# The first pair's z in 32-row products, with the stack for the rest sent by DMA

## Chip, cores and metric

One core of one Trainium2 chip. The metric is the device time of one execution in microseconds (us). Names of engines: PE is TensorE's matmul stream and PEld its weight loads, DVE is VectorE, ACT is ScalarE, POOL is GpSimd, SP is SyncE, which here only issues DMAs.

## What is computed

Three layers in a row; only the third is touched by the change, and the second hands it its input.

```python
x = attention(q, k, v)                       # 2304 rows of 512
# second layer, "moe": 8 experts x 4 slots
logits = x @ phi                             # 2304 x 32
slot_input = softmax_over_rows(logits).T @ x # 32 x 512
slot_out[e] = relu(slot_input[e] @ w1[e]) @ w2[e]
x = softmax_over_slots(logits) @ slot_out    # = c @ slot_out
# third layer, "moe2": 8 experts, every row through every expert
P = exp(x @ w_gate - max); 8 rounds of row and column normalisation
for e in range(8):
    out += P[:, e:e+1] * (relu(x @ w1[e]) @ w2[e])
```

## The kernel before

The input of the third layer is never formed. Since x = c @ slot_out, the product x @ m1[e] is c @ (slot_out @ m1[e]): `prep_w1(e)` multiplies the transposed slot outputs `st` (32 columns) into m1[e], scales the 32 x 1024 result by a power of two and splits it into two f16 parts, `sh` (high) and `sl` (low). These lie as 128 x 256: four groups of 32 partitions (kk), each with 256 of the 1024 columns. `stk[e]`, the stack, is 128 x 1024 f16: rows sh, sh, sl, sl of 32 each, which is the operand that PE loads as weights. `ct` holds the split and transposed c in the matching row order (hi, lo, hi, lo), so that one 128-row product sums all four cross products. `emit_z(m, fh)` makes z for a pair m of row tiles (n and n + 9) and half fh of the 1024 columns: 4 matmuls of 256 columns into a PSUM tile of two banks.

For e of 1 and more the stack is filled by 16 small DMAs from SP (L765, 32 partitions x 512 B each). For e = 0 it is made on PE: 8 products with selection matrices `selh`, `sell` (L774), 3 idle products (L777), and four copies out of PSUM by ACT and DVE (L779).

After z, each pair has seven products (Strassen style): `hi_z`, `lo_z`, `relu_z`, `sum_z`, `hi_s` and `lo_s` read z (or sums of it) and write the f16 operands `ops`; `prod` is then 12 matmuls of 256 columns (L1149) over one operand. The order on PE is written out by hand: for pair 0 it is KA11 (high part), KA12 (high part), KA11 (low part), the matmuls of `first_w1` (m1[1], L721), KA12 (low part), KS2, z of pair 1 (first half), KS3, z of pair 1 (second half), KS1, KA22, then KA11 of pair 1, KS4 of pair 0, and so on. `left(m + 1, k_)` puts the work of ACT, DVE and POOL on the next pair behind step k_ of this one; `side` does the same for the preparation of the next expert: `magnitude(1)` with eight ACT passes over m2[1] (L605), `prep_w1(1)`, the gate and its normalisation. Every engine takes its instructions in this order. `add` on ACT copies x out of PSUM between two products that accumulate in the same x, so the later product waits for that copy.

Loads come by SP alone. `load_part` sends 2 MB of m1[1] and of m2[1] into `wraw` (L67) as the last two loads ahead of the main loop. The tile framework puts all semaphores, those of the DMAs' landings included.

The lines that the change touches: L491 to L501 (`constants`), L716 to L781 (`prep_w1`), L890 to L895 (`ct_turn`), L947 to L980 (end of the second layer and `prep_w1(0)`), L996 to L1000 (`gate`), L1255 to L1325 (start of the main loop).

Of the kernel before, what the change touches and what calls it, by code (L numbers as in the profile page):

```python
# [26 lines left out]
def tile_kernel(ctx: ExitStack, tc: tile.TileContext, q, k, v, phi, w1, w2, w_gate, m1, m2, rel, out):  # L27
    nc = tc.nc
# [71 lines left out]
    with tc.manual_schedule():  # L100
        with ExitStack() as ab:
# [8 lines left out]
            with ExitStack() as at:  # L110
# [380 lines left out]
                id16, selh, sell = [ring[:, 8, 256 + 64 * i:320 + 64 * i].bitcast(F16) for i in range(3)]  # L491

                def constants():
                    nc.gpsimd.tensor_copy(out=id16, in_=idn)
                    nc.gpsimd.memset(selh, 0.0)
                    nc.gpsimd.memset(sell, 0.0)
                    for i in range(4):
                        for cp in range(4):
                            dst = selh if cp < 2 else sell
                            nc.gpsimd.tensor_copy(out=dst[32 * i:32 * i + 32, 32 * cp:32 * cp + 32],  # L500
                                                  in_=idn[32 * i:32 * i + 32, 32 * i:32 * i + 32])  # L501
# [91 lines left out]
            bound = {}  # L593

# [121 lines left out]
            def prep_w1(e, ps=None, pool=None, beside=None, behind=None, last=None):  # L716
# [22 lines left out]
                ar = mp.tile([128, 1], F32, tag="ar1", name="ar1")  # L739
                nc.vector.tensor_reduce(out=ar, in_=ps[:, 256:384 if e else 385], axis=AX.X, op=ALU.max)  # L740
# [5 lines left out]
                if e == 0:  # L746
                    last(0)
                nc.vector.tensor_single_scalar(inv_s[:, e:e + 1].bitcast(I32), ar.bitcast(I32), 0x7F800000,
                                               op=ALU.bitwise_and)
# [5 lines left out]
                if e == 1:  # L755
                    yield
                nc.vector.scalar_tensor_tensor(out=sl, in0=ps[:, 0:256], scalar=iv, in1=sh,
                                               op0=ALU.mult, op1=ALU.subtract)
                yield
                yield  # L760
                stk[e] = (sp if e % 2 else mp).tile([128, F], F16, tag="stk", name="stk", bufs=1)
                if e:
                    for i, part in enumerate((sh, sh, sl, sl)):
                        for kk in range(4):
                            nc.sync.dma_start(out=stk[e][32 * i:32 * i + 32, 256 * kk:256 * kk + 256],  # L765
                                              in_=part[32 * kk:32 * kk + 32, :])
                    yield
                    return
                last(1)
                pss = [pool.tile([128, 512], F32, tag="b", name="m") for _ in range(4)]  # L770
                for lhs, rhs in ((selh, sh), (sell, sl)):
                    for kk in range(4):
                        rows = slice(32 * kk, 32 * kk + 32)
                        nc.tensor.matmul(pss[kk][:, 0:256], lhsT=lhs[rows], rhs=rhs[rows], start=lhs is selh,  # L774
                                         stop=lhs is sell, tile_position=(32 * kk, 0))
                for _ in range(3):
                    nc.tensor.matmul(pss[3][:, 256:512], lhsT=id16, rhs=ct.rearrange("p a b -> p (a b)")[:, 0:256], start=True, stop=True)  # L777
                for kk in range(4):
                    (nc.vector.tensor_copy if kk % 2 else nc.scalar.copy)(  # L779
                        out=stk[e][:, 256 * kk:256 * kk + 256], in_=pss[kk][:, 0:256])  # L780
                yield  # L781

            with ExitStack() as bs:
# [106 lines left out]
                def ct_turn(g, copy=nc.vector.tensor_copy):  # L890
                    n = min(4, NT - 4 * g)
                    ps = pb.tile([128, 4, 128], F16, tag="b", name="bc")
                    for i in range(n):
                        nc.tensor.transpose(ps[:, i, :], ct[:, 4 * g + i, :], id16)
                    return lambda: copy(out=ct[:, 4 * g:4 * g + n, :], in_=ps[:, 0:n, :])  # L895
# [9 lines left out]
                for e in range(E):  # L905
                    mm1(e)
                    for _ in range((2, 4, 2, 2, 0, 1, 0, 0)[e]):
                        next(p2)
                    if e == 0:
                        slots()  # L910
                    if e == EH - 1:
                        tr1_out(0)
                    if e == EH + 1:
                        for g in range(NG):
                            ct_split(g)
                    if e == EH + 2:
# [30 lines left out]
                for h in range(2):  # L947
                    for fc in range(FC):
                        mm2(E - 1, fc, h)
                    (nc.scalar.copy if h else nc.vector.tensor_copy)(  # L950
                        out=s2b[:, 256 * h:256 * h + 256], in_=s2[h][:, 0:256])
                pc = pm.tile([128, 512], F32, name="m")
                turned, later = [], []
                for h in range(2):
# [6 lines left out]
                    if h == 0:  # L961
                        turned.append(ct_turn(0))
                turned.pop()()

                def beside():
                    turned.append(ct_turn(2))
                    later.append(cn_turn(pc, 0, 2))

                def behind():
                    turned.pop()()  # L970
                    turned.extend((ct_turn(1, nc.scalar.copy), ct_turn(3), ct_turn(4)))
                    later.append(cn_turn(pc, 2, 4))
                    later.append(cn_turn(s2[0][:, 256:512], 4, 5))
# [5 lines left out]
                for _ in prep_w1(0, ph, pb, beside, behind, last):  # L979
                    pass  # L980
# [3 lines left out]
            with ExitStack() as ms:  # L984
# [9 lines left out]
                def gate():  # L994

                    st4 = sp.tile([128, DC, 4, NS], F32, name="st4")  # L996
# [3 lines left out]
                    nc.vector.tensor_copy(out=st4, in_=st.unsqueeze(2).to_broadcast([128, DC, 4, NS]))  # L1000
# [65 lines left out]

                def emit_z(m, fh):
                    e, n = divmod(m, NP)
                    if fh == 0:
                        pool = wcv if m % 2 == 0 else wone  # L1070
                        ops_[m] = pool.tile([128, 7, 2, 4, 128], F16, tag="w", name="ops")
# [183 lines left out]
                load_part("m1", 1, wraw, 0, 1)  # L1255
                load_part("m2", 1, wraw, 0, 1)
                emit_z(0, 0)
                emit_z(0, 1)
# [13 lines left out]
                lo_z(0, KA12, 1, 2)  # L1272
                xt[0] = px.tile([128, 256], F32, tag="x", name="x")
# [6 lines left out]
                hi_s(0, KS3, "s3")  # L1280
                lo_s(0, KS3, "s3")
                lo_s(0, KS2, "s2", nc.vector)
                sum_z(0, "s1", 2, 2, "r21", ALU.add)
                sum_z(0, "s4", 1, 2, "s2", ALU.subtract)
                prod(0, KA12, yt[0][:, 0], True, (1,))
                side = None
                for m in range(NM):
# [12 lines left out]
                    for k_ in range(7):  # L1300
# [18 lines left out]
                        if k_ == 0:  # L1319
                            if m:  # L1320
                                last(m - 1)
                            left(m, 7)
# [72 lines left out]
```

## Time and profile before

| | us |
|---|---|
| median of 3 runs | 909.25 (908.68 to 910.03) |
| the profiled execution | 909.3 |
| its span, first to last instruction | 907.5 |
| PE busy | 894.7 (99%) |
| DVE, ACT, POOL busy | 673.3, 583.1, 562.6 |

The stretch that the change touches lies between 151 us, where the second layer's last matmul ends, and 180 us. Times of rows are counted from the start of the span. From about 177 us on, PE runs without a gap to the end, so an amount by which that point moves is an amount by which the end moves.

### The profile page before, as it was taken

How to read it: one execution, taken by the hardware profiler on the slowest of the kernel's cores; microseconds unless marked ns; L12 is line 12 of the kernel's file. 1: busy time of each engine (PE TensorE's matmuls, PEld its weight loads, DVE VectorE, ACT ScalarE, POOL GpSimd, SP SyncE). 2: the span in 40 equal slices, each digit the busy share in tenths (PEclk: the TensorE clock that was granted, in tenths of full speed). 3: DMA queues.
4: the chain of work that ended last, by engine and by line, in shares of the span. 5: the costliest groups of instructions: out<-in, count | busy, mean ns of one | idle time of the engine just before them, and what ended most of it. 6: DMA issues, size and time to landing. Idle time of an engine off the chain costs nothing.

```text
span 907.5 us, 24182 instructions
## 1 busy us (share of the span) xinstructions
PE 894.7 (99%) x9604; PEld 772.2 (85%) x9604; DVE 673.3 (74%) x1627; ACT 583.1 (64%) x1322; POOL 562.6 (62%) x716
## 2 busy tenths in 40 slices
PE   8999999999999999999999999999999999999998
PEld 6777765888888888888888888888888888888887
DVE  6666668688867777777787778777777777777775
ACT  7777655767768785766476656665666666664442
POOL 2111233458865996598659874997489848894452
PEclk9999999999999999999999999999999999999999
DMA  9999999120022002300230023001300020002222
GB/s 299 357 333 325 323 410 423 65 99 1 2 98 101 1 1 97 104 1 2 94 105 2 2 93 106 1 1 58 142 1 2 17 90 2 2 1 48 47 48 70
DMA packets 33632, 90.16 MB, mean 99 GB/s; under 512 B 5360, under 2 KB 9712, under 8 KB 30192
## 3 DMA queue, kind: packets, MB, share of 16 engines
q1 hardware_dynamic: 33296, 88.30, 27.7%
q8 instruction: 75, 1.23, 0.6%
q14 instruction: 37, 0.30, 0.1%
q10 hardware_dynamic: 224, 0.33, 0.1%
HBM read 82.05 MB, written 4.72 MB: 96 GB/s over the span
## 4 chain that ended last, share of the span: by engine, by line
PE 92%; DMA 3%; DVE 2%; ACT 2%; issue 1%; POOL 0%; SPq 0%; DVEq 0%; ACTq 0%
PE x L1149 41%; PE y L1149 31%; PE z L1075 7%; PE xp L246 3%; DMA w<-in_moe_w_dram 3%; PE s L178 2%; PE pt L222 2%; PE m L721 1%; PE pt L280 1%; PE pt L291 1%; ACT et L208 1%; PE h L839 1%; DVE et L199 1%; PE ps L331 0%; DMA rel_sb<-in_alibi_dram 0%
## 5 line engine op out<-in xcount | busy, mean ns | idle before, releaser
L1149 PEld LDWEIGHTS <-ops 128*128 128x128 f16 x6048 | 591.8, 98 | 69.1 <-issue 0.6
L1107 POOL TENSOR_TENSOR ops<-s,ops 128x512 f16<-128x512 f32 x287 | 332.5, 1160 | 217.2 <-ACT ops L1104 215.9
L1149 PE MATMUL x<-w2h,ops 128*128 128x256 f16 x2304 | 413.1, 273 | 0.1
L1149 PE MATMUL y<-w2h,ops 128*128 128x256 f16 x1728 | 318.3, 273 | 0.0
L1149 PE MATMUL x<-w2l,ops 128*128 128x256 f16 x1152 | 313.3, 273 | 0.0
L1104 ACT CAST ops<-s 128x512 f16<-128x512 f32 x288 | 177.9, 618 | 206.8 <-DVE s L1100 204.7
L1149 PE MATMUL y<-w2l,ops 128*128 128x256 f16 x864 | 235.0, 273 | 0.0
L1163 DVE SCALAR_TENSOR_TENSOR acc<-x,pe,acc 128x256 f32<-128x256 f32 x252 | 121.6, 483 | 78.8 <-PE x L1149 77.4
L1085 ACT ACTIVATE ops<-z 128x512 f16<-128x512 f32 x216 | 128.6, 595 | 37.1 <-PE z L1075 34.3
L1088 DVE SCALAR_TENSOR_TENSOR ops<-z,ops 128x512 f16<-128x512 f32 x216 | 146.7, 679 | 0.0
L1163 DVE SCALAR_TENSOR_TENSOR acc<-y,pe,acc 128x256 f32<-128x256 f32 x189 | 91.3, 483 | 64.8 <-PE y L1149 64.8
L678 POOL TENSOR_TENSOR w2l<-w,w2h 128x256 f16<-128x256 f32 x168 | 112.6, 674 | 0.0
L1100 DVE SCALAR_TENSOR_TENSOR s<-z,r 128x512 f32<-128x512 f32 x144 | 98.0, 681 | 8.8 <-ACT r L1096 6.1
L1100 DVE SCALAR_TENSOR_TENSOR s<-z,s 128x512 f32<-128x512 f32 x144 | 97.9, 680 | 1.3 <-issue 1.0
L1075 PE MATMUL z<-ct,stk 128*128 128x256 f16 x576 | 86.3, 273 | 0.6 <-DVE stk L779 0.5
L681 ACT CAST w2h<-w 128x256 f16<-128x256 f32 x168 | 67.5, 402 | 0.5 <-POOL w L678 0.5
L1075 PEld LDWEIGHTS <-stk 128*128 128x128 f16 x576 | 55.7, 98 | 10.1 <-issue 2.9
L208 ACT ACTIVATE et<-et,mx 128x192 f32<-128x192 f32 (+2 forms) x144 | 51.1, 426 | 19.4 <-DVE mx L199 19.2
L485 POOL TENSOR_TENSOR w<-mx 128x1 f32<-128x1 f32 x72 | 11.9, 193 | 82.3 <-DVE mx L199 82.3
L199 DVE CUSTOM_DVE_ANT_0 et<-s,rel_sb 128x192 f32<-128x192 f32 (+2 forms) x144 | 39.6, 331 | 22.2 <-PE s L178 19.7
L1096 ACT ACTIVATE r<-z 128x512 f32<-128x512 f32 x72 | 42.4, 589 | 0.0
L605 ACT ACTIVATE t<-w 128x512 f32<-128x512 f32 x64 | 40.4, 631 | 0.8 <-PE pf L439 0.4
(224 smaller groups left out, 744.8 us busy)
## 6 DMA issues: line engine op xcount, KB each, us to landing
w<-in_moe_w_dram SPq DMA_DIRECT2D x14, 2048.0 KB, 8.3
w<-in_moe_w_dram SPq DMA_DIRECT2D x72, 256.0 KB, 5.2
w<-in_moe_w_dram SPq DMA_DIRECT2D x12, 1024.0 KB, 9.0
kT<-in_k_dram SPq DMA_DIRECT2D x18, 256.0 KB, 5.3
qT<-in_q_dram SPq DMA_DIRECT2D x17, 256.0 KB, 5.3
v<-in_v_dram SPq DMA_DIRECT2D x16, 260.0 KB, 5.4
w<-in_moe_w_dram SPq DMA_DIRECT2D x8, 512.0 KB, 11.1
out_dram<-acc SPq DMA_DIRECT2D x32, 128.0 KB, 2.3
```

The lines of the kernel that those rows point to most:

```text
L199: nc.vector.tensor_tensor_reduce(out=runs[hh], in0=ps[j][:, gg, col:192], in1=rel_sb[:, 2 * hf + gg, col:192], scale=-0.125, scalar=3e38, ...
L208: nc.scalar.activation(out=runs[hh], in_=runs[hh], func=AF.Exp, bias=mx[:, hh:hh + 1], scale=-1.0)
L678: nc.gpsimd.tensor_tensor(out=out_, in0=x_, in1=y_, op=ALU.subtract)
L681: nc.scalar.copy(out=hi[:, i, r], in_=src[:, r])
L1075: nc.tensor.matmul(ps[:, i], lhsT=stk[e][:, 128 * ft:128 * ft + 128], rhs=ct.rearrange("p (a n) t -> p a n t", a=2)[:, :, n, :], start=Tru ...
L1085: nc.scalar.activation(out=ops_[m][:, k_, 0], in_=zb(m, i, j), func=AF.Relu)
L1088: nc.vector.scalar_tensor_tensor(out=ops_[m][:, k_, 1], in0=zb(m, i, j), scalar=0.0, in1=ops_[m][:, k_, 0], op0=ALU.max, op1=ALU.subtract)
L1100: nc.vector.scalar_tensor_tensor(out=new_sum(m, nm), in0=zb(m, i, j), scalar=0.0, in1=o, op0=ALU.max, op1=op)
L1104: nc.scalar.copy(out=ops_[m][:, k_, 0], in_=sm_[m, nm])
L1107: eng.tensor_tensor(out=ops_[m][:, k_, 1], in0=sm_[m, nm], in1=ops_[m][:, k_, 0], op=ALU.subtract)
L1149: nc.tensor.matmul(out_, lhsT=a_[:, k_, l_, i, :], rhs=r_[:, k_, i, :], start=(first and j == 0), stop=(j == len(todo) - 1 and 1 in parts) ...
L1163: nc.vector.scalar_tensor_tensor(out=o, in0=ps, scalar=pe_[e][:, t:t + 1], in1=o, op0=ALU.mult, op1=ALU.add)
```

## The change

- z of pair 0 is made by `emit_z0` straight from `sh` and `sl`: 24 products of 32 rows, four row groups side by side, into two PSUM tiles of two banks each. Three of the four cross products are made (low times low is left out). The other operand is `ctr`, a copy of c's split for the two row tiles of pair 0 with each part repeated in four row groups; POOL writes it early (`spread`) and `ct_turn(-1)` turns it.
- stk[0] is sent by the 16 DMAs of L765 as for the other experts; the selection matrices, the products L774 and L777 and the copies L779 are gone. The loads of m1[1] and m2[1] stand ahead of these DMAs on SP.
- Both halves of `s2b` are copied by ScalarE (before: one by VectorE).
- The gate's operand `st4` is made right behind `st`, in `s2b`'s buffer, instead of behind z.
- The turns of `ct` are dealt out anew: groups 0 and 2 beside the maximum, 1 and 4 behind it into banks of `s2`, 3 behind KA12 of pair 0; all are copied by VectorE.
- For pair 0, `lo_z` KA11, `hi_z` KA22, `hi_s`/`lo_s` KS3 and `lo_z` KA22 come earlier; the m1[1] products come ahead of KA11's low part; the first half of pair 1's z comes behind KS3 instead of behind KS2.

```diff
@@ prep_w1
-                if e:
-                    for i, part in enumerate((sh, sh, sl, sl)):
-                        for kk in range(4):
-                            nc.sync.dma_start(out=stk[e][32 * i:32 * i + 32, 256 * kk:256 * kk + 256],
-                                              in_=part[32 * kk:32 * kk + 32, :])
-                    yield
-                    return
-                last(1)
-                pss = [pool.tile([128, 512], F32, tag="b", name="m") for _ in range(4)]
-                for lhs, rhs in ((selh, sh), (sell, sl)):
-                    for kk in range(4):
-                        rows = slice(32 * kk, 32 * kk + 32)
-                        nc.tensor.matmul(pss[kk][:, 0:256], lhsT=lhs[rows], rhs=rhs[rows], start=lhs is selh,
-                                         stop=lhs is sell, tile_position=(32 * kk, 0))
-                for _ in range(3):
-                    nc.tensor.matmul(pss[3][:, 256:512], lhsT=id16, rhs=..., start=True, stop=True)
-                for kk in range(4):
-                    (nc.vector.tensor_copy if kk % 2 else nc.scalar.copy)(
-                        out=stk[e][:, 256 * kk:256 * kk + 256], in_=pss[kk][:, 0:256])
+                for i, part in enumerate((sh, sh, sl, sl)):
+                    for kk in range(4):
+                        nc.sync.dma_start(out=stk[e][32 * i:32 * i + 32, 256 * kk:256 * kk + 256],
+                                          in_=part[32 * kk:32 * kk + 32, :])
@@ end of the second layer
+                def spread():
+                    for h in range(2):
+                        nc.gpsimd.tensor_copy(
+                            out=ctr[:, 2 * h:2 * h + 2].rearrange("p a (r s) -> p a r s", r=4),
+                            in_=ct.rearrange("p (a n) t -> p a n t", a=2)[:, :, 0, 32 * h:32 * h + 32].unsqueeze(2).to_broadcast(
+                                [128, 2, 4, NS]))
...
-                    (nc.scalar.copy if h else nc.vector.tensor_copy)(
+                    nc.scalar.copy(
                         out=s2b[:, 256 * h:256 * h + 256], in_=s2[h][:, 0:256])
...
+                load_part("m1", 1, wraw, 0, 1)
+                load_part("m2", 1, wraw, 0, 1)
-                for _ in prep_w1(0, ph, pb, beside, behind, last):
+                for _ in prep_w1(0, ph, beside, behind, last):
@@ main loop
+                def emit_z0():
+                    new_ops(0)
+                    for fh in range(2):
+                        zt[0, fh] = pz.tile([128, 4, 2, 128], F32, tag="z", name="z")
+                    for x_, (h, r_, c) in enumerate(((0, 0, 0), (0, 1, 0), (0, 0, 1), (0, 1, 1), (1, 0, 0), (1, 0, 1))):
+                        for kk in range(4):
+                            rows = slice(32 * kk, 32 * kk + 32)
+                            nc.tensor.matmul(zt[0, kk // 2][:, 2 * (kk % 2) + c], lhsT=shl[h][rows, 128 * c:128 * c + 128],
+                                             rhs=ctr[rows, 2 * r_:2 * r_ + 2], start=(x_ == 0), stop=(h == 1),
+                                             skip_group_check=True, tile_position=(32 * kk, 0))
...
                 hi_z(0, KA11, 1, 1)
+                lo_z(0, KA11, 1, 1)
+                hi_z(0, KA12, 1, 2)
                 relu_z(0)
-                hi_z(0, KA12, 1, 2)
+                hi_z(0, KA22, 2, 2)
                 sum_z(0, "s3", 1, 1, "r21", ALU.subtract)
-                lo_z(0, KA11, 1, 1)
+                hi_s(0, KS3, "s3")
+                lo_s(0, KS3, "s3")
...
                 prod(0, KA11, xt[0], True, (0,))
                 prod(0, KA12, yt[0][:, 0], True, (0,))
+                ct_turn(3, ct3)()
+                next(first_w1)
                 prod(0, KA11, xt[0], True, (1,))
-                next(first_w1)
                 nc.scalar.copy(out=acc[:, 0, 0:256], in_=xt[0])
...
                             step(m, 0)
-                            hi_z(0, KA22, 2, 2)
                             hi_s(0, KS1, "s1")
                             lo_s(0, KS1, "s1")
-                            emit_z(m + 1, 0)
                             step(m, 1)
                             step(m, 2)
+                            emit_z(m + 1, 0)
```

## Rows read from the trace of the kernel before

**Rows 1.** The chain of waits that ended last: start, us, what.

```profile
127.32 11.10 DMA w<-in_moe_w_dram
...
138.48 0.33 SPq L67
...
138.90 15.64 DMA w<-in_moe_w_dram
...
157.51 0.50 DVE sl L757
...
159.29 1.03 PE z L1075 x8
...
177.59 1.31 PE y L1149 x12
```

**Rows 2.** Busy time by engine in one stretch, then clock, DMA share, GB/s.

```profile
158.00:160.00 2.00, 1.44 (x14) 1.04 (x14) 1.18 (x3) 0.90 (x5) 0.00 (x0) 1.00 0.97 418
```

**Rows 3.** Timeline around pair 0's z: start, us, engine, line, operation.

```profile
156.52 0.59 ACT L895 COPY ct<-bc 128x512 f16<-128x512 f16 x1 [3.25 <-PE bc L894]
156.62 0.15 DVE L744 TENSOR_SCALAR w1i<-ar 128x1 int32<-128x1 int32 x1
157.00 0.48 ACT L754 ACTIVATE sh<-h,w1i 128x256 f16<-128x256 f32 x1
157.53 0.29 PE L774 MATMUL m<-sh,kT 32*128 32x256 f16 x4 [0.38 <-ACT sh L754]
158.77 0.10 PEld L1075 LDWEIGHTS <-stk 128*128 128x128 f16 x1 [0.28 <-ACT stk L779]
159.92 0.60 ACT L1085 ACTIVATE ops<-z 128x512 f16<-128x512 f32 x1 [0.93 <-PE z L1075]
160.16 0.96 PE L1004 MATMUL m<-wg_sb,st 128*128 128x8 f32 x8
160.97 0.27 PE L1149 MATMUL x<-w2h,ops 128*128 128x256 f16 x1
```

**Rows 4.** Timeline of PE behind it: m1[1], pair 1's z, KS1, pair 2's z.

```profile
163.25 1.93 PE L721 MATMUL m<-w,st 128*32 128x256 f32 x32
...
166.87 0.60 PE L1075 MATMUL z<-ct,stk 128*128 128x256 f16 x4
...
169.24 0.27 PE L1149 MATMUL y<-w2h,ops 128*128 128x256 f16 x1
...
176.98 0.61 PE L1075 MATMUL z<-ct,stk 128*128 128x256 f16 x4
```

**Rows 5.** Timeline of ACT and DVE on pair 1's operands.

```profile
167.07 0.37 ACT L1159 COPY acc<-x 128x256 f32<-128x256 f32 x1 [0.43 <-PE x L1149]
...
167.96 0.59 ACT L1085 ACTIVATE ops<-z 128x512 f16<-128x512 f32 x1
...
169.69 0.63 ACT L1085 ACTIVATE ops<-z 128x512 f16<-128x512 f32 x1
...
176.25 0.68 DVE L1088 SCALAR_TENSOR_TENSOR ops<-z,ops 128x512 f16<-128x512 f32 x1
```

**Rows 6.** Timeline of SP's DMA issues.

```profile
127.80 0.44 SPq L849 DMA_DIRECT2D wg_sb<-in_moe_w_gate_dram  x1
128.67 22.95 SPq L67 DMA_DIRECT2D w<-in_moe_w_dram  x10
...
179.78 4.96 SPq L765 DMA_DIRECT2D stk<-sl  x8
```

**Rows 7.** Landing of loads issued at 144 to 146, at 151.2 to 151.6.

```profile
w<-in_moe_w_dram SPq DMA_DIRECT2D x1, 2048.0 KB, 14.5
...
w<-in_moe_w_dram SPq DMA_DIRECT2D x1, 2048.0 KB, 12.9
```

**Rows 8.** The stack's DMAs (L765): ns of an issue, us to landing, min/median/max.

```profile
L765 SPq DMA_DIRECT2D stk<-sl x56: 528/588/1516, 179.8 to 741.5; - x56
...
DMA to landing us min/median/max: 1.7/1.8/3.8
```

More of the change, by code (lines that the diff above doesn't have):

```diff
@@ L490, in tile_kernel @@
                 sc_ = ring[:, 8].rearrange("p (c t) -> p c t", c=DC)
-                id16, selh, sell = [ring[:, 8, 256 + 64 * i:320 + 64 * i].bitcast(F16) for i in range(3)]
+                id16 = ring[:, 8, 256:320].bitcast(F16)
                 def constants():
                     nc.gpsimd.tensor_copy(out=id16, in_=idn)
[L495 to L501, printed above, removed]
                 def turned():
@@ L714, in prep_w2a, with prep_w1 @@
                 yield
-            def prep_w1(e, ps=None, pool=None, beside=None, behind=None, last=None):
+            def prep_w1(e, ps=None, beside=None, behind=None, last=None):
                 if e:
@@ L758, in prep_w1 @@
                                                op0=ALU.mult, op1=ALU.subtract)
+                if e == 0:
+                    last(1)
+                    exponent()
+                    shl.extend((sh, sl))
                 yield
@@ L888, in ct_split, with ct_turn @@
                                                        op0=ALU.mult, op1=ALU.subtract)
[L890 removed]
+                ctr = ring[:, 8, 0:256].bitcast(F16).rearrange("p (q t) -> p q t", q=4)
+                def ct_turn(g, at_=None):
                     n = min(4, NT - 4 * g)
[L892 removed]
+                    src = ctr if g < 0 else ct[:, 4 * g:4 * g + n, :]
+                    n = src.shape[1]
+                    ps = (pb.tile([128, 4, 128], F16, tag="b", name="bc") if at_ is None else
+                          at_.bitcast(F16).rearrange("p (q t) -> p q t", q=n))
                     for i in range(n):
[L894 to L895 removed]
+                        nc.tensor.transpose(ps[:, i, :], src[:, i, :], id16)
+                    return lambda: nc.vector.tensor_copy(out=src, in_=ps[:, 0:n, :])
+                def spread():
[4 more added lines that the diff above has]
+                                [128, 2, 4, NS]))
                 def cn_turn(ps, g0, g1):
@@ L915, in tile_kernel @@
                             ct_split(g)
+                        spread()
                     if e == EH + 2:
@@ L961, in tile_kernel, with behind @@
                     if h == 0:
-                        turned.append(ct_turn(0))
+                        turned.append(ct_turn(-1))
                 turned.pop()()
+                st4 = s2b[:, 0:512].rearrange("p (a b c) -> p a b c", a=DC, b=4)
+                nc.vector.tensor_copy(out=st4, in_=st.unsqueeze(2).to_broadcast([128, DC, 4, NS]))
                 def beside():
-                    turned.append(ct_turn(2))
+                    turned.extend((ct_turn(0), ct_turn(2)))
+                def behind():
+                    turned.pop(0)()
                     later.append(cn_turn(pc, 0, 2))
-                def behind():
-                    turned.pop()()
-                    turned.extend((ct_turn(1, nc.scalar.copy), ct_turn(3), ct_turn(4)))
+                    later.append(ct_turn(1, s2[1][:, 0:256]))
                     later.append(cn_turn(pc, 2, 4))
-                    later.append(cn_turn(s2[0][:, 256:512], 4, 5))
+                    later.append(cn_turn(s2[0][:, 384:512], 4, 5))
+                    later.append(ct_turn(4, s2[0][:, 256:384]))
                 def last(i):
@@ L1284, in tile_kernel @@
                 sum_z(0, "s4", 1, 2, "s2", ALU.subtract)
+                lo_z(0, KA22, 2, 2)
                 prod(0, KA12, yt[0][:, 0], True, (1,))
@@ L1321, in tile_kernel @@
                                 last(m - 1)
-                            left(m, 7)
+                                left(m, 7)
                         next(side, None)
```

24 lines of the change are left out of this document (11 added, 13 removed).

## Prediction

> **What bounds the kernel now.** I read the busy shares first: PE is busy for 99% of the span, so only stretches where it stalls, or works on something else's account, can be won. The chain of waits shows where that is. Up to 154.54 us it is one run of loads: a DMA from 127.32 to 138.42, then one issued at 138.90 that lands 15.64 us later [rows 1]. That last one is m1[0]'s final quarter, and the DMA share is still 0.97 after it [rows 2], because m1[1] and m2[1] stand behind it. So whatever the change does ahead of 154.54 (both `s2b` copies on ACT, `st4` early, `spread` on POOL, no selection matrices) waits for the same landing; I cost it at nothing. If that landing came sooner, an `st` that is ready earlier could count by about one such copy, 0.37 [rows 5].
>
> From 154.54 to about 161 the chain is the making of the stack: `sl` at 157.51, z at 159.29 [rows 1], the first product at 160.97 [rows 3]. From there PE is full to 167, and then something else leads: pair 1's operands. ACT starts the first (`hi_z`) at 167.96, the second z half's at 169.69 [rows 5], and works through that pair's list in its fixed order; the last reader of pair 1's z, DVE's `lo_z` KA22 at 176.25 to 176.93 [rows 5], lets pair 2's z start at 176.98 [rows 4]. Behind that PE has no gap. So the end moves by as much as **the start of pair 1's operands** moves, and the question is when pair 1's z is there.
>
> **Part by part: z of pair 0.** `w1i` is ready at 156.77; `sh` started only at 157.00 behind ACT's copy of ct [rows 3], which the change gives to DVE. So `sh` runs 156.80 to 157.28 (gain 0.2; the bounds are 0 and that copy's 0.59). `sl` follows to 157.79 at its old length [rows 1]. The 24 products: four of 32 rows side by side took 0.29 together, no more than one [rows 3], so six rounds at 0.109 each (12 matmuls of 256 columns take 1.31 [rows 1]). The four rounds on `sh` hide behind `sl`; the two on `sl` run 157.83 to 158.05. If they did not overlap at all, they would take 24 x 0.109 = 2.6, and z would be some 1.9 later, which the wait below would just swallow. ACT's first `hi_z` starts at 158.24 (last product's start + 0.27 + 0.03) instead of 159.92. The eight gate matmuls, 0.81 from 160.16 to 160.97 [rows 3], run 158.05 to 158.86, so the first product starts at about 158.95: **2.0 us earlier** than before.
>
> **The products of pair 0.** From 158.95 on PE: KA11 high 0.87, KA12 high 0.87, the moved turn of ct's group 3 (4 transposes of half the columns, about 0.25; at most 0.44), the 32 matmuls on m1[1] 1.9 [rows 4], KA11 low 0.44: 163.25. m1[1] has landed by 146 + 14.5 = 160.5 at the latest [rows 7], in time for 160.94. Now the reordering costs: KS2 must wait for ACT's copy of x (0.37 [rows 5], with latencies 163.43 to 163.80), covered by KA12 low but for 0.2. KS2 runs 163.85 to 165.16. KS3 accumulates in the same x and must wait for the next such copy, 165.35 to 165.72. Before, pair 1's z half filled that gap; now nothing does, 0.6 is lost, and KS3 runs 165.77 to 167.08. The operands are there: `lo_z` KA11 on DVE to 159.6, `relu_z` at the latest behind it, to 160.2, s3 to 160.9, s2 to 161.6, KS2's parts by 163.3, at 0.6 to 0.7 each as in [rows 3, 5]. So PE is ready for pair 1's first z half at 167.08; before it ran at 166.87 [rows 4]. The 2.0 us are spent, in part on KS3 in front. If the stack were there for nothing, this half would end for ACT at 167.7, and pair 1's operands would start 0.2 earlier than before: **that is the most that the change can win.**
>
> **The stack by DMA.** It does not come for nothing. SP issues sixteen DMAs, each about 0.62 behind the last (eight in 4.96, of which the last 0.59 [rows 6]), landing 1.8 after issue [rows 8]. First I look at how SP issues at all. Its loads show a hold: the load issued at 127.32 lands at 138.42, and SP issues a later load at 138.48, 0.06 behind that landing [rows 1]. Counting issues from 127.32: wg_sb at 127.80 is the first behind it, then ten up to 151.6 [rows 6], of which 138.48 and 138.90 are the seventh and eighth (only those at 144.92 and 151.29 come later). So 138.48 is the **eighth** behind 127.32, and 138.90 the eighth behind wg_sb. I read this as eight landing semaphores that take turns, SP not issuing on one whose last DMA is still under way.
>
> The last load ahead of the stack is m2[1], issued at 151.29, landing 12.9 later, at 164.2 [rows 7]. The eighth DMA behind it is the stack's eighth. The first seven go out from 157.35 to about 161.1 (the seventh has m1[1]'s semaphore, landed by then). The eighth waits, though ready at 161.7, until 164.2, and the other eight behind it: SP takes its queue in order. From 164.24 at 0.624 each: 13th 167.36, 14th 167.98, 15th 168.61, 16th 169.23; landing 1.8 later at 169.16, 169.78, 170.41, 171.03. The sixteen go by row group, four column blocks in each, so the first column block is whole with the 13th, the second with the 14th, and so on.
>
> **The sum.** Pair 1's first z half needs blocks one and two: its last two matmuls start 0.14 (weights and latency) behind 169.78, at 169.92 and 170.03, end 0.27 later, and ACT's `hi_z` starts at 170.33 instead of 167.96: **+2.37**. The second half needs block four: to 171.55, ready for ACT's 1.73 later at 172.06. KS1 starts at 171.39 instead of 169.24 [rows 4], +2.15, so PE comes no later than the operands. ACT's list behind that is the same as before (one of its eight passes over m2[1] slips in front of `hi_z`, as before), so pair 2's z moves by 2.37 and the end with it. The profiled execution of before, 909.3, stands within 0.1 of the median, 909.25. **909.25 + 2.37 = 911.6.** PE reaches the wait 2 us before the stack, so errors in pair 0's products don't enter while they stay under that.
>
> Bounds of this case: issues of 0.53 to 0.59 [rows 8] take up to 0.4 off the six that count, a landing of 1.7 another 0.1, and before's own runs spread by 0.6 down and 0.8 up: 910.5 to 912.4. One landing of 3.8 instead of 1.8 [rows 8] adds up to 2.0, to 913.6; it is the longest of all and I leave it out.
>
> **Rivals.**
> 1. *SP is not held* (0.13): the DMAs are issued through and only queue behind m2[1] on the engines. The Trainium skill's page "DMA: Bandwidth & Descriptors" (Queues, rings and completion order) has descriptors taken in ring order, and by that alone this would be the result: small transfers wait for m2[1], issues don't. Against it: the 0.06 after 138.42, where nothing else ended. Its time from rows: 14th issued at 157.35 + 13 x 0.624 = 165.46, landed 167.26, 16th 168.51; `hi_z` at 167.8 to 168.2 for a pitch up to 0.65; -0.15 to +0.3, so **909.3**, no change. This is the side that is not slower; it decides by whether the eighth stack DMA goes out before 162 or behind 164.2. Even here there is no gain over 0.2.
> 2. *z waits for all sixteen* (0.08): if the wait of pair 1's z is on the whole stack, its first matmul starts at 171.17 and `hi_z` at 171.8, +3.84, **913.1**. Against it: before, z's first weights load at 158.77, behind the first of the four copies into the stack and ahead of the last [rows 3].
> 3. *The clock falls* (0.03): PE would idle for 2 us at 167, with 8 matmuls in the 2 after it. Before, the granted clock is 1.00 (2.4 GHz) also where PE is busy for 1.44 of 2 us [rows 2], but no such hole is shown. At 1.2 GHz the four products from KS1 to KS4, 4 x 1.31 [rows 1], would take twice as long, at worst +5.2, some **917**.
> 4. *Something ahead of z wins more than I see* (0.02): the loads would have to come earlier, against 0.97 of DMA share; below 907.4.
>
> **How the numbers follow.** The forecast has 0.74. About 0.2% (1.8 us, so 911.07) is what a measurement of this kernel can tell from no change. Slower by more: most of the forecast (0.68) and rivals 2 and 3, 0.79. Within: rival 1 and the forecast's lower end, 0.19. Faster: 0.02. The range 910.5 to 913.2 holds the forecast and rival 2, a good 0.8; rival 1 is left out below.
>
> **What would show it.** In the profile after: `hi_z` of pair 0 at about 158.2 and the first product at 159 (step one); pair 0's KS3 behind an idle 0.6 (step two); SP's eighth stack DMA at 164.2 with nothing issued in the 2.5 us before; an idle PE of 2 us ended by a landing of the stack, z of pair 1 in pieces up to 171.5, pair 2's z near 179.4. I am wrong if the stack's issues run through without a hole (rival 1), or if pair 2's z comes at 177 or before.

## The result, and the profile after

The changed kernel takes **915.81 us** (median of 6 runs) beside 909.32 for the kernel before on the same chip: a ratio of 1.0067 (95% interval 1.0053 to 1.008), so slower, by less than 1%. The forecast was 911.6, in a range up to 913.2. Its sign was right, and its size too small by more than the range: the time went where the working had put down nothing.

The profiled execution after has a span of 913.2 us, 5.7 more than before. The change's own numbers are the best way in. In the stretch that I had costed at nothing, the longest waits of POOL and PE between 120 and 158 us that the kernel before does not have are these (who waits <- for whom: us in total, times, longest; a longer one, of POOL for L827, is there before too):

```profile
POOL kT L893 <- DVE ct L875: 5.3, 1, 5.3
PE b L847 <- DVE hsb L840: 5.0, 1, 5.0
```

L893 is `spread` (its operand lies in a buffer that the trace calls kT); L847 turns `hsb`, the sums of the first products, for the second. How they hang together is read from POOL's order. Before, on POOL (start, us, engine, line, operation; in brackets the idle time in front and who ended it):

```profile
127.99 2.52 POOL L654 TENSOR_TENSOR t<-w 128x512 f32<-128x512 f32 x2 [2.03 <-ACT t L605]
...
136.98 4.46 POOL L654 TENSOR_TENSOR w<-w,t 128x512 f32<-128x512 f32 x2 [3.99 <-DVE w2l L639]
```

And after (L654 is now L648):

```profile
128.50 0.40 POOL L893 COPY kT<-ct 128x256 f16<-128x256 f16 x1 [2.97 <-ACT ct L873]
134.18 1.07 POOL L893 COPY kT<-ct 128x256 f16<-128x256 f16 x1 [5.27 <-DVE ct L875]
135.22 2.71 POOL L648 TENSOR_TENSOR t<-w 128x512 f32<-128x512 f32 x2
...
140.71 2.85 POOL L648 TENSOR_TENSOR w<-w,t 128x512 f32<-128x512 f32 x2
```

`spread` stands on POOL ahead of the differences of w2's blocks. Its second copy reads the low parts of `ct` (the remainders that the f16 high parts leave), which VectorE makes only from 133.0 on. POOL takes its list in order, so the differences that ran from 128.0 now run from 135.2. The VectorE rows that answer to each other, before and then after, each with the start of the low parts of `ct` in front:

```profile
133.50 1.97 DVE L887 SCALAR_TENSOR_TENSOR ct<-cn,ct 128x128 f16<-128x128 f32 x10
...
136.03 2.85 DVE L639 SCALAR_TENSOR_TENSOR w2l<-w,w2i,w2h 128x256 f16<-128x256 f32 x7
138.81 0.41 DVE L852 COPY hsb<-h 128x256 f32<-128x256 f32 x1
```

```profile
133.03 1.96 DVE L875 SCALAR_TENSOR_TENSOR ct<-cn,ct 128x128 f16<-128x128 f32 x10
...
135.56 8.67 DVE L633 SCALAR_TENSOR_TENSOR w2l<-w,w2i,w2h 128x256 f16<-128x256 f32 x7
144.16 0.41 DVE L840 COPY hsb<-h 128x256 f32<-128x256 f32 x1
```

The same seven low parts of w2 take 2.85 us before and 8.67 after, 0.41 and 1.24 each. Before, POOL was idle when VectorE began them; after, VectorE and POOL take turns, one of POOL's differences (2.85 for two) to one low part. The Trainium skill's page "SBUF — State Buffer" (SBUF: two separate sides) says of the port pair that VectorE and GpSimd share that it is an exclusive lock: of a GpSimd operation that reads SBUF and a VectorE operation with two inputs in SBUF, as a low part has, whichever starts first holds it for its whole instruction. The trace agrees, with 1.42 us from one low part to the next beside POOL; no run here changes the port alone. The low parts also read ScalarE's high parts, but the first eight of those were done by 136.57, so the seven did not wait for them:

```profile
133.27 3.30 ACT L640 ACTIVATE w2h<-w,w2i 128x256 f16<-128x256 f32 x8 [3.93 <-issue]
```

The copy of `hsb` stands behind the seven in VectorE's order, and TensorE behind `hsb`. TensorE and its clock (columns of the second fence: stretch, busy us and count of PE, PEld, DVE, ACT, POOL, then granted clock, DMA share, GB/s):

```profile
144.62 0.69 PE L847 MATMUL b<-idn,hsb 128*128 128x128 f32 x2 [5.05 <-DVE hsb L840]
145.24 1.08 PE L928 MATMUL s<-w 128*32 128x256 f32 x8
...
158.51 1.93 PE L715 MATMUL h<-w,st 128*32 128x256 f32 x32
...
162.62 0.62 PE L1083 MATMUL z<-kT,sh 32*128 32x256 f16 x16 [0.26 <-ACT sh L753]
163.14 0.40 PE L1083 MATMUL z<-kT,sl 32*128 32x256 f16 x8
...
164.38 0.27 PE L1168 MATMUL x<-w2h,ops 128*128 128x256 f16 x1
...
171.31 0.27 PE L1168 MATMUL x<-w2h,ops 128*128 128x256 f16 x1 [0.46 <-ACT acc L1178]
...
172.63 0.38 PE L1094 MATMUL z<-ct,stk 128*128 128x256 f16 x2
173.20 0.39 PE L1094 MATMUL z<-ct,stk 128*128 128x256 f16 x2 [0.19 <-DMA stk<-sl]
...
182.67 0.61 PE L1094 MATMUL z<-ct,stk 128*128 128x256 f16 x4
```

```profile
136.00:140.00 4.00, 3.57 (x68) 1.90 (x60) 4.00 (x4) 1.20 (x4) 4.00 (x4) 1.00 1.02 418
140.00:144.00 4.00, 0.00 (x0) 0.00 (x0) 4.00 (x4) 1.19 (x3) 3.58 (x4) 0.70 1.00 414
144.00:148.00 4.00, 3.38 (x30) 1.67 (x34) 4.00 (x7) 2.87 (x14) 2.74 (x2) 0.50 1.01 417
```

TensorE stands still for 5.05 us up to 144.62; in that hole the granted clock falls to 0.5 (1.2 GHz), and the second products begin at half pace (1.08 for eight; at full pace 0.61 to 0.62). They end at 157.4 instead of 151.2. Between them and the end of m1[0]'s products stand the turn of their sums (1.1 us) and those products themselves (1.93), 3.1 in all, where the kernel before took 4.0, since it waited for the load that landed at 154.54:

```profile
152.95 2.27 PE L721 MATMUL h<-w,st 128*32 128x256 f32 x32
```

So 1.0 of the 6.2 us is swallowed by that wait, and m1[0]'s products end at 160.44 instead of 155.22. From there my own steps can be read. ACT (to be held beside [rows 3, 5]) and SP (beside [rows 6]):

```profile
162.09 0.47 ACT L753 ACTIVATE sh<-h,w1i 128x256 f16<-128x256 f32 x1 [3.26 <-DVE w1i L743]
...
163.57 1.09 ACT L1104 ACTIVATE ops<-z 128x512 f16<-128x512 f32 x2 [0.30 <-PE z L1083]
...
173.63 0.60 ACT L1104 ACTIVATE ops<-z 128x512 f16<-128x512 f32 x1 [1.76 <-PE z L1094]
```

```profile
157.49 0.33 SPq L67 DMA_DIRECT2D w<-in_moe_w_dram  x1
162.59 5.55 SPq L767 DMA_DIRECT2D stk<-sh  x8
168.24 4.97 SPq L767 DMA_DIRECT2D stk<-sl  x8
```

I cut the path into three pieces, the same in every kernel below: **A**, from the start of VectorE's low parts of `ct` (133.50 before, 133.03 after) to the end of m1[0]'s products; **B**, from there to pair 0's first product; **C**, from there to pair 1's `hi_z`. Before: A 21.73, B 5.75, C 6.99. After: A 27.41, B 3.94, C 9.25. The differences are +5.68, -1.81 and +2.26, in sum +6.1. The ratio makes 6.1 us, with 4.8 to 7.3. B is the gain by the direct z, C the price of the new order (0.35 of it a wait for the stack between the first two pairs of z products); A is what I left out. From pair 1's `hi_z` to the end the profiled executions of before and after take the same 739.5 to 739.6 us.

### The profile page after: what moved, and what is told of

It reads as the page before. It is cut to its first block, busy times and chain, and to the rows that moved or that the text cites. A ratio compares the mean times of both kernels' runs of the same rounds, so it can differ in the third digit from the quotient of the medians.

```text
span 913.2 us, 24207 instructions
## 1 busy us (share of the span) xinstructions
PE 896.3 (98%) x9613; PEld 772.1 (85%) x9613; DVE 675.2 (74%) x1626; ACT 583.3 (64%) x1320; POOL 560.0 (61%) x700
## 4 chain that ended last, share of the span: by engine, by line
PE 80%; DVE 0%; issue 0%
PE x L1168 40%; PE y L1168 31%; PE z L1094 7%; PE m L715 1%; PE m L591 0%; PE m L1017 0%; PE m L1043 0%; DVE ops L1107 0%; DVE acc L1182 0%; DVE acc L1180 0%
## 5 line engine op out<-in xcount | busy, mean ns | idle before, releaser
L672 POOL TENSOR_TENSOR w<-w 128x256 f32<-128x256 f32 x56 | 40.9, 730 | 0.0
## 6 DMA issues: line engine op xcount, KB each, us to landing
w<-in_moe_w_dram SPq DMA_DIRECT2D x8, 512.0 KB, 11.1
out_dram<-acc SPq DMA_DIRECT2D x32, 128.0 KB, 2.3
```

The source lines that it names most:

```text
L672: nc.gpsimd.tensor_tensor(out=out_, in0=x_, in1=y_, op=ALU.subtract)
```

## The experiments

Times are against the kernel before in the same runs; the difference in us is the ratio less one by 909 to 910. Clock: where the granted clock fell to 1.2 GHz between 125 and 190 us.

| kernel | A | B | C | A+B+C against before | clock 1.2 GHz | measured, 95% |
|---|---|---|---|---|---|---|
| before | 21.73 | 5.75 | 6.99 | 0 | never | 0 |
| the change | 27.41 | 3.94 | 9.25 | +6.1 | 141.6 to 148.5 | +6.1 (4.8 to 7.3) |
| before_spread | 26.93 | 5.75 | 6.99 | +5.2 | 144.0 to 147.4 | +5.2 (3.4 to 7.1) |
| before_spread_hi | 22.43 | 5.75 | 6.99 | +0.7 | never | +0.5 (-0.2 to 1.4) |
| after_warm | 25.62 | 3.94 | 9.18 | +4.3 | never | +4.5 (2.8 to 6.1) |
| hsb_early | 24.77 | 4.40 | 9.27 | +4.0 | 156.8 to 160.2 | +3.6 (2.3 to 5.0) |
| hsb_early_half | 23.81 | 3.94 | 9.21 | +2.5 | never | +4.1 (2.7 to 5.4) |
| spread_late | 21.03 | 3.94 | 11.75 | +2.3 | 172.2 to 175.6 | +4.1 (2.8 to 5.5) |
| late_warm | 21.32 | 3.94 | 11.70 | +2.5 | never | +2.9 (1.8 to 3.9) |
| late_m2_pool | 22.75 | 3.93 | 10.65 | +2.9 | never | +2.1 (0.5 to 3.6) |
| late_half | 21.11 | 3.94 | 9.58 | +0.2 | never | +0.3 (-0.6 to 1.3) |
| late_half_z | 22.13 | 3.94 | 9.23 | +0.8 | 169.4 to 172.8 | +0.4 (-1.0 to 1.7) |
| v2 | 21.23 | 3.94 | 7.44 | -1.9 | 170.3 to 173.7 | +0.7 (-0.3 to 1.8) |
| v1 | 21.01 | 3.94 | 7.44 | -2.1 | never | -1.4 (-2.2 to -0.6) |

A clock that falls, or a wait that comes, behind pair 1's `hi_z` is in the last column and not in the sum: that is how spread_late, v2 and late_half_z are to be read (740.5, 743.5 and 741.1 us from that `hi_z` to the end). A, B and C come from one profiled execution of each kernel, the last column from all executions.

**Is it `spread`, and is it its place?** spread_late moves it behind the last conversions of w2:

```diff
                     if e == EH + 1:
                         for g in range(NG):
                             ct_split(g)
-                        spread()
...
                 for _ in p2:
                     pass
+                spread()
```

> The changed kernel with one edit: both POOL copies that make ctr stand behind all differences that POOL forms for the second weights, instead of ahead of them. Theory (POOL's queue): the second copy waits for VectorE's low parts and holds up the differences behind it; without that, the 5.05 us hole of PE at 139.6 is gone, the clock stays at 1.00, the second layer's last matmul ends at 151.2 again, and the end part runs as forecast: the eighth stack DMA waits for m2[1] to land at 164.2, pair 1's first hi_z at 170.3, 911.6 us. Rival (the loss is in the end part): the hole stays or the time stays, 915 us.

The hole at 139.6 is gone, A is 21.03, and the differences on POOL start where they did. What comes up in its place is the wait that the forecast was about. SP, then TensorE, then the clock:

```profile
151.50 0.33 SPq L67 DMA_DIRECT2D w<-in_moe_w_dram  x1
```

```profile
160.32 1.22 SPq L767 DMA_DIRECT2D stk<-sh  x2
```

```profile
164.70 0.51 SPq L767 DMA_DIRECT2D stk<-sh  x1
```

```profile
169.71 0.38 PE L1094 MATMUL z<-ct,stk 128*128 128x256 f16 x2 [2.32 <-DMA stk<-sl]
...
171.55 0.39 PE L1094 MATMUL z<-ct,stk 128*128 128x256 f16 x2 [0.31 <-DMA stk<-sl]
```

```profile
172.00:174.00 2.00, 2.00 (x13) 1.50 (x11) 1.16 (x2) 2.00 (x6) 1.16 (x1) 0.54 0.01 4
```

Seven stack DMAs go out up to 160.95; the eighth, at 164.70, goes out just behind m2[1]'s landing (164.69, 13.2 us after its issue); the profile puts 3.1 us of SP's waiting there down to that load. TensorE then waits 2.32 us for the stack, and 2.5 us after that wait the clock falls, for 3.4 us. So the theory of the place holds, but the time is +4.1 us where 911.6 meant +2.3; the clock, below, is what it lacked.

**`spread` alone.** before_spread is the kernel before with `spread` put where the change has it, its result read by nobody; before_spread_hi has the same two copies, both from the high part, which ACT makes first (L885, from 127.9). The first change below is what both add (with the definition of `spread`), the second is what before_spread_hi has instead of before_spread.

```diff
                         for g in range(NG):
                             ct_split(g)
+                        spread()
...
-                            in_=ct.rearrange(...)[:, :, 0, 32 * h:32 * h + 32]...
+                            in_=ct.rearrange(...)[:, :, 0, 0:32]...
```

> The kernel before with the two POOL copies that make ctr added at the place where the change has them; nothing reads the result. Theory (POOL's queue): the hole of 5 us and the lower clock come here too, the last matmul of the second layer ends at 157.4, the products on m1[0] end at 160.4 instead of 155.2, 914.5 us. Rival (the loss comes from the end part): no change, 909.3.

> The kernel before with two copies of the same shape and place on POOL as in before_spread, but both read the high part of the hidden state, so that neither waits for VectorE's low parts; nothing reads their result. Theory (before_spread lost 5.0 us since the second copy's wait for the low parts, ending at 134.2, held the differences behind it in POOL's queue): the differences start within 1.5 us of the kernel before, the hole of TensorE at 139.6 is under 1.5 us, and the time is within 0 and +1.0 us of the kernel before. Rival (the copies' own work on POOL or its port shared with VectorE makes the loss): +4 to +5 us as in before_spread.

POOL in before_spread_hi:

```profile
129.03 0.74 POOL L902 COPY kT<-ct 128x256 f16<-128x256 f16 x2 [3.00 <-ACT ct L885]
129.73 2.52 POOL L654 TENSOR_TENSOR t<-w 128x512 f32<-128x512 f32 x2
...
138.07 4.47 POOL L654 TENSOR_TENSOR w<-w,t 128x512 f32<-128x512 f32 x2 [3.35 <-DVE w2l L639]
```

With the wait, the kernel before loses 5.2 us and shows the hole of 5.1 and the fall of the clock; without it the difference is 0.5 us and can't be told from none. So it is the wait inside POOL's queue, and not the copies' own work (0.74 us), that makes the loss. (In before_spread the profile puts the 5.3 us in front of the second copy down to a load, in the change to VectorE. The copy starts 0.06 to 0.07 behind the end of VectorE's fifth low part in both, at 134.10 and 134.18, and before_spread_hi, with the same loads, has no such wait.)

**How much of it is the clock?** after_warm gives TensorE twenty products of 128 columns in fp32, read by nobody, ahead of L847.

```diff
+                        warm(pb, "b", ones, 20, 128)
```

> The changed kernel with 20 idle matmuls (128 columns, f32, some 4.4 us) on PE where its hole of 5 us is, ahead of the second turn of hsb. Theory (the hole also costs the clock): the clock stays at 1.00, the 32 matmuls behind the hole take 1.7 us instead of 3.3, and 1.6 us come back: 914.2. Rival (those matmuls were covered by loads): 915.8.

The clock stays at 1.00 and A is 1.8 shorter than with the change; the times differ by 1.6, though their intervals overlap. So some 1.8 of the 5.7 in A are the clock, by the one profiled execution of each.

**The way from POOL to TensorE.** hsb_early puts VectorE's copy of `hsb` ahead of the last four steps of w2's preparation; hsb_early_half has the split load of late_half (below) as well.

```diff
+                    if e == E - 1:
+                        tr1_out(1)
                     for _ in range((0, 0, 0, 0, 0, 2, 4, 4)[e]):
                         next(p2)
-                tr1_out(1)
```

> The change with one step of VectorE's order altered: the copy hsb of the second half's products stands ahead of the last four steps of w2's preparation instead of behind them; spread stays where the change has it, so POOL's differences are as late as in the profile after. Theory (the hole of 5.05 us is made by VectorE: seven low parts of w2 in front of hsb in its queue last 1.4 instead of 0.4 us each, since they run beside POOL's late differences): the low parts stay as slow, but hsb runs within 1 us of the end of the first products at 139.6, TensorE's hole there is under 1.5 us, the clock stays at 1.00 in it, the second products end by 152.5, and what is left is the hold of the stack's eighth DMA as in spread_late: +3 to +4.2 us against the kernel before. Rival (POOL's lateness stops TensorE in another way too, by the high parts on ScalarE or by POOL's own work): a hole of 3 us or more stays ahead of the second products, +5 to +6.5 us as with the change.

> hsb_early with the load of m2[1] in two halves, the second behind the stack's DMAs, as in late_half. Theory (with the hole and the hold both gone nothing of the change's loss is left, though spread is early and POOL late): -0.3 to +1.2 us against the kernel before. Rival (late differences cost elsewhere): +2 us or more.

The link is confirmed: `hsb` now stands behind three slow low parts, and the hole is 0.44 us instead of 5.05. But the loss did not go with it. VectorE in hsb_early:

```profile
136.58 4.05 DVE L633 SCALAR_TENSOR_TENSOR w2l<-w,w2i,w2h 128x256 f16<-128x256 f32 x3
140.56 0.41 DVE L840 COPY hsb<-h 128x256 f32<-128x256 f32 x1
140.89 10.05 DVE L633 SCALAR_TENSOR_TENSOR w2l<-w,w2i,w2h 128x256 f16<-128x256 f32 x13
...
152.45 3.24 DVE L633 SCALAR_TENSOR_TENSOR w2l<-w,w2i,w2h 128x256 f16<-128x256 f32 x8
155.63 0.25 DVE L962 COPY st<-b 128x64 f32<-128x64 f32 x1
```

The slow low parts are a backlog on VectorE, and the next copy behind it, `st` at 155.63 (before: 152.41), keeps m1[0]'s products waiting for 1.6 us. hsb_early has the time that I expected for another reason than I gave: its stack was not held (the eighth DMA at 166.41, m2[1] landed at 164.23). hsb_early_half goes against my theory and with its rival: the late differences cost in two places, and the earlier of them hides the later. Of its +4.1 the profile shows +2.5; the profiled execution took 912.24, the median is 914.05, and what the other executions lost besides (their mean clock is 0.997 to 0.998 beside 0.999 in the profiled one) is open.

**The hold of the eighth DMA.** All have `spread` late. late_m2_pool gives m2[1]'s load to POOL's queue; late_half splits it, the second half behind the stack's DMAs:

```diff
-                load_part("m2", 1, wraw, 0, 1)
+                load_part("m2", 1, wraw, 0, 2)
                 for _ in prep_w1(0, ph, beside, behind, last):
                     pass
+                load_part("m2", 1, wraw, 1, 2)
```

late_m2_pool, in `load_part`:

```diff
-        nc.sync.dma_start(out=t[:, n0:n1], in_=src[:, n0:n1])
+        (nc.gpsimd if (nm, e) == ("m2", 1) else nc.sync).dma_start(out=t[:, n0:n1], in_=src[:, n0:n1])
```

> The kernel above (ctr's copies late) with the load of m2[1] issued from POOL's queue, so that it takes none of the eight landing semaphores of SP's DMAs. Theory (SP is held by the semaphore of m2[1]): the sixteen stack DMAs go out from 157.4 to 167.2 without a hole, pair 1's first hi_z at 167.8 to 168.2, 909.1 to 909.5 us. Rival (the stack only queues behind m2[1] on the DMA engines, or its sixteen issues alone set the time): the same time as the kernel above, 911.6.

The time of late_m2_pool, +2.1 where I expected none, says nothing about the hold: both loads were under way together, m1[1] landed only at 164.20, and its products waited 1.2 us for it. SP's issues show the turn of eight all the same. The eighth stack DMA, now the one on m1[1]'s semaphore, goes out at 164.86, when that load has landed; the ninth goes out at 166.17, just behind the landing of the first (166.1), which had lain behind both loads, and the profile puts 0.7 us of SP's waiting down to that.

> The change with spread moved behind the last conversions (as in spread_late) and the load of m2[1] issued in two halves, the second behind the stack's sixteen DMAs. Theory (the eighth DMA of the stack is held until the load that used the same landing semaphore eight issues earlier has landed; in spread_late 164.69, issue 164.70): the first half lands about 162, the stack's DMAs go out without a hole of over 1 us, the blocks of pair 1 land about 2.5 us earlier than in spread_late (167.0 instead of 169.57), hi_z of pair 1 starts at 168.0 to 168.4 (kernel before: 167.96), no 2 us hole on TensorE, granted clock 1.00 all through, and the time is within -0.3 and +0.6 us of the kernel before. Rival (the stack is late for the queue's own pace or the DMA engines' load): landings within 0.7 us of spread_late's, and the time is +3 to +4 us as there.

```profile
159.72 5.87 SPq L767 DMA_DIRECT2D stk<-sh  x8
165.69 4.97 SPq L767 DMA_DIRECT2D stk<-sl  x8
170.71 0.58 SPq L67 DMA_DIRECT2D w<-in_moe_w_dram  x1
```

Everything in this execution lies 2.5 us later than in spread_late, from a slower start of the program (granted clock 0.50 from 8 to 14 us). Eight issues take 5.87 instead of 8.05, C falls from 11.75 to 9.58, and the time is the kernel before's. The Trainium skill's page "DMA: Bandwidth & Descriptors" (Queues, rings and completion order) says that each DMA engine takes its descriptors in ring order. The trace agrees for the transfers: the first stack DMA of spread_late, behind m2[1], takes 7.7 us to land. By that rule alone an issue would not have waited; 164.70 in spread_late shows that SP's issue itself does.

**How much of spread_late is the clock?** late_warm is spread_late with nine idle products of 128 columns ahead of pair 1's z.

```diff
                             step(m, 2)
+                            for _ in range(9):
+                                nc.tensor.matmul(yt[0][:, 1, 0:128], lhsT=ones, rhs=ones, start=True, stop=True)
                             emit_z(m + 1, 0)
```

> spread_late with nine products of 128 columns in fp32, whose results nobody reads, put ahead of the z products of pair 1, so that TensorE has work in the 2.3 us in which it waits for the stack. Theory (of spread_late's +3.7 us the hold of the eighth DMA makes 2.4, and the fall of the clock to 1.2 GHz from 172.16 to 175.58 the rest): granted clock 1.00 all through, hi_z of pair 1 where spread_late has it (170.3 to 170.7), and the time is +2.2 to +2.8 us over the kernel before. Rival (the clock's fall costs nothing, since TensorE then waits less elsewhere): +3.4 to +4 as in spread_late.

```profile
166.64 2.17 PE L1333 MATMUL y<-ones 128*128 128x128 f32 x18
169.07 0.38 PE L1094 MATMUL z<-ct,stk 128*128 128x256 f16 x2 [0.26 <-DMA stk<-sl]
```

The z products of pair 1 come as late as in spread_late, the clock stays, C is the same (11.70), and the time is +2.9 instead of +4.1: the hold is worth about the 2.4 that the forecast gave it, the clock by these times another 1.2, though their intervals overlap; in the two profiled executions it is 0.7 (from pair 1's `hi_z` to the end 740.5 us in spread_late, 739.8 in late_warm).

**Where would the direct z pay?** v1 is late_half with the stack's DMAs ordered by blocks (0, 1, 3, 2, block 3's issued by POOL), and pair 1's first z half back behind the second sum's steps. v2 leaves all sixteen to SP, in the order 0, 1, 2, 3; late_half_z has only the last two changed lines below.

```diff
+                four = list(enumerate((sh, sh, sl, sl)))
+                for i, kk, part in ([(i, kk, p_) for kk in (0, 1, 3, 2) for i, p_ in four] if e == 0 else
+                                    [(i, kk, p_) for i, p_ in four for kk in range(4)]):
+                    (nc.gpsimd if e == 0 and kk == 3 else nc.sync).dma_start(
...
+                            emit_z(m + 1, 0)
                             step(m, 1)
                             step(m, 2)
-                            emit_z(m + 1, 0)
```

> late_half with the stack's DMAs ordered by blocks (all four quarters of block 0, then of block 1, 3 and 2), block 3's issued by POOL, and the z products of pair 1's first half back behind the second sum's steps, where the kernel before has them. Theory: TensorE's path has the z of pair 0 about 2 us earlier than in the kernel before, and with the stack's first blocks landing about 165 that gain is no longer eaten: hi_z of pair 1 at 165.8 to 166.6 (kernel before: 167.96), and the time is -1.2 to -2.2 us. Rival (the stack by DMA cannot be there before about 168 whatever the order of issue): hi_z of pair 1 at 167.9 or later and the time within 0.5 us of the kernel before, or over it.

> v1 with all sixteen DMAs of pair 1's stack issued by SP, block by block, none by POOL. Theory (a DMA of this kind costs SP 0.63 us, so sixteen of them last 10 us): the first two blocks are there as in v1 and the z products of pair 1's first half start as there, 8.1 us behind the first product of pair 0's z; the last block lands 12 us behind it where v1 needs it at 10.0, so TensorE waits 1.5 to 2 us at the second half, and the time is 1.2 to 1.8 us over v1: -0.3 to +0.4 us against the kernel before. Rival (only the first half's time counts, the second has room): the time of v1, -1.2 to -2 us.

> late_half with nothing else than the z products of pair 1's first half back behind the second sum's steps, the stack's DMAs in the order of the change (by quarters). Theory (the first half needs the 13th and the 14th DMA, which land 10.9 us behind the first product of pair 0's z, 2.7 us after TensorE comes to it): a hole of 2.3 to 3 us ahead of these products, after which the clock may fall, and the time is +0.5 to +2.5 us against the kernel before. Rival (the place of these products in TensorE's order alone makes v1's gain): -1 us or less.

v1, TensorE and ACT:

```profile
164.81 0.60 PE L1171 MATMUL x<-w2h,ops 128*128 128x256 f16 x4
165.25 0.60 PE L1097 MATMUL z<-ct,stk 128*128 128x256 f16 x4
...
167.18 0.60 PE L1097 MATMUL z<-ct,stk 128*128 128x256 f16 x4
```

```profile
166.35 0.59 ACT L1107 ACTIVATE ops<-z 128x512 f16<-128x512 f32 x1
```

Neither half of pair 1's z waits, and the kernel takes 908.35 us, ratio 0.9985 (0.9976 to 0.9993): faster than both kernels. v2 has the first half as early and waits for the last block, in the waits between 156 and 174 us:

```profile
PE z L1097 <- DMA stk<-sl: 2.9, 1, 2.9
```

I had expected 1.5 to 2 there, and a time of 1.2 to 1.8 over v1's, where it is 2.1 by the two ratios; the last DMA landed 13.1 us behind the first z product, not 12, and the clock fell too. late_half_z waits 1.7 us at the first half (I had expected 2.3 to 3), and its clock falls as well. So the order of the products alone is not enough, and with the DMAs by blocks it is not enough either while SP issues all sixteen; the blocks' order without that of the products was not run.

## Why the prediction was wrong, point by point

- **What failed** is the sentence of the first part that costs everything ahead of 154.54 at nothing, "`spread` on POOL" among it. The stretch that I named as the one that the change touches, from 151 us on, leaves out the place where `spread` runs (128.5 to 135.2). The bound was read rightly: loads did end the wait at 154.5. But a bound covers a delay only up to its slack, which was 1.0 us here (the 3.4 from 151.2 to 154.5, less what has to be done in between anyway), and I neither wrote down that slack nor asked what was queued behind `spread`. One look at POOL's list shows the differences of w2 behind it, and one at VectorE's list the low parts of `ct` (from 133.5) that its second half reads. What the runs showed in place of the nothing: +5.68 in A, 1.8 of it the clock.
- **B, the direct z**: 2.0 earlier forecast, 1.81 measured, and within 0.01 of that in every kernel that has it but hsb_early, where the clock was down (1.35). `hi_z` of pair 0 starts 0.30 behind the last z product, as told.
- **C, the products' order**: PE ready for pair 1's z 8.13 behind the first product forecast (167.08 - 158.95), 8.25 measured (172.63 - 164.38). The stall ahead of KS3 was put at 0.6 and took 0.46.
- **The hold**: the mechanism was right, and where the cover of A is gone it has the forecast size: eighth DMA at 164.70 (164.2 forecast), and +2.3 to +2.5 in A+B+C beside the +2.37. In the changed kernel itself it doesn't bind. The stack's first DMA goes out at 162.59, so that the eighth comes after m2[1]'s landing (issued at 157.49, 7.8 us under way), and the z products wait 0.2 to 0.3 a piece. What I named as the sign of it, an idle PE of 2 us, is therefore not in the profile after, and rival 1's sign (issues without a hole) is, though rival 1 is wrong. So the right sign of the forecast is luck: in this kernel the wait that it stood on is not there, B and C together make only +0.45, and the loss has another source.
- **The translation into time**: pair 1's `hi_z` 5.67 later (173.63 against 167.96), pair 2's z 5.69 later (182.67 against 176.98), the span 5.7. That ACT's fixed order carries a late start unchanged to the end held to 0.03.
- **Rival 3, the clock**, had 0.03, far too little: after a hole of 2.3 us in the place that I named, the clock did fall (spread_late), at a cost of 0.7 to 1.2 us and not the 5.2 of its worst case. That the clock stays at 1.00 where PE is busy for 1.44 of 2 us [rows 2] said nothing about an unbroken hole.
- **"The most that the change can win" is 0.2**: true of the order that it has; with `spread` late, the load split, the stack by blocks and the old place of the z half, v1 keeps 1.4 us.

## What to carry to other kernels

A piece of work given to an idle engine costs what stands behind it in that engine's list: for each such piece, ask for its latest operand, not only for its duration, and follow the delay through the engines that share a port or a list with it. Where a bound covers an edit, write down the slack of the cover (here 1.0 us), since the rest of a delay comes through. And when two costs lie one behind the other, each hides the other: take the first away, look again, and only then speak of the second's size.

## What the runs showed of the hardware

- Beside POOL's subtractions of 512 columns in fp32, VectorE's low parts of 256 columns came every 1.42 us instead of every 0.40 in the batch that POOL began (135.22 after); when VectorE was first (136.03 before), POOL's two took 4.46 instead of 2.5 to 2.9 us.
- Between 125 and 190 us the granted clock fell to 1.2 GHz in holes of TensorE of 5.05 us (2.1 us into it in the changed kernel, 0.6 ahead of its end in before_spread) and 2.9 us (0.6 ahead of its end, v2), behind holes of 2.3 (spread_late) and 1.7 us (late_half_z), and in hsb_early behind one of 1.1 and one of 1.6 us whose ends lie 2.9 us apart. It stayed at 2.4 GHz through holes of 1.3 and 1.2 us (late_m2_pool), through two of 1.3 us whose ends lie 4.0 apart (hsb_early_half), and where idle products filled the long ones. Each fall lasted 3.4 us, that in the changed kernel 6.8.
- An SBUF to SBUF DMA of 16 KB costs SP 0.63 us to issue and lands 1.8 us later (the median; 7.7 where m2[1] lay ahead of it). Sixteen took 10.6 to 11.1 us of SP's time where no issue was held, in each order that was run (after, late_half, late_half_z, v2); with four of them on POOL's queue SP was done in 8.0 (v1).
